# Leaky-ReLU taken twice from the PSUM accumulator by ScalarE, and GpSimd's elementwise work given to VectorE, in a dynamic convolution followed by two MLPs

## The chip, the cores and the metric

One NeuronCore of a Trainium2 chip runs the whole program in one launch. The metric is the device time of that launch in microseconds; the program before was run three times.

## The reference

```python
# local sum: softmax over 7 taps per token and head, then a causal weighted sum
w = exp(weight_gen - max(weight_gen, -1)); w = w / (sum(w, -1) + 1e-9)
x_pad = concatenate([zeros(B, 6, D), x], axis=1)
out = einsum('bshk,bskhg->bshg', w, x_unf)       # B=2, S=4096, D=192, 8 heads, 7 taps
x = out.reshape(8192, 192)
# first MLP: leaky ReLU with slope 0.01
h = x @ moe_w_in;  g = maximum(0.01 * h, h);  x = g @ moe_w_out       # 192 -> 2048 -> 192
# second MLP: squared ReLU
h = x @ moe2_w_in; r = maximum(h, 0); g = r * r; out = g @ moe2_w_out # 192 -> 2048 -> 192
```

The weights arrive as float64 words, and are turned into float32 on the core.

## The kernel before, in words

**Tiles.** The 8192 tokens are worked in 16 blocks of 512 (`NTB`), the 2048 hidden features in 16 slices of 128 (`NFC`). A *step* is one block and one slice of one layer: 512 steps in all. A *phase* is the 16 steps of one block in one layer. The phases run in the order layer 1 block 0 (steps 0 to 15), layer 1 block 1 (16 to 31), layer 2 block 0 (32 to 47), layer 1 block 2 (48 to 63), layer 2 block 1, and so on alternately. In the code layer 1 is `l == 0`.

**Exact halves.** Each float32 operand v of a product is split into two float32r halves: h is v rounded, and lo is v minus h. Products are summed as h*h + h*lo + lo*h.

**One step.** `mm1` (L376) makes the hidden slice in a PSUM tile `ph` (two buffers) by five matmuls. `act_a` applies the activation: in layer 1 ScalarE copies `ph` to `g` (L383) and VectorE replaces `g` by max(0.01 g, g) (L384); in layer 2 ScalarE does Relu from `ph` and Square in place (L386, L387). One step later `act_b` makes the two halves: `gh`, a rounding copy of `g`, on ScalarE (L395) or VectorE (L397), swapped for the steps listed in `GH_SWAP`; and `gl = g - gh` (L398) on VectorE, or on GpSimd for the 35 steps in `GL_POOL`, all below step 44. Three steps after the activation (`LAG`) `mm2` (L411 to L415 for layer 1, L425 and L428 for layer 2) multiplies `gh` and `gl` by the output weights. `g` has three buffers, `gh` and `gl` four.

**The weights.** 28 pieces of weights (14 a layer; kinds a, b of the input matrix and o of the output matrix) are prepared among steps 0 to 45, at the steps in `DUE`. A piece is loaded by DMA; ScalarE scales its high words (`scale`, L138); VectorE joins them by four instructions (`join`: L151, L154, L155, L147) and an add (L148) that is VectorE's or GpSimd's by the table `ENGINES`; then `split` makes the halves: h by ScalarE or VectorE (L163), lo = v minus h by VectorE or GpSimd (L164). The three numbers of a piece in `ENGINES` are for the add, lo and h; 0 is GpSimd for the first two and ScalarE for the third, 1 is VectorE.

**The local sum.** Of each of the first three blocks (`POOL_TAPS`) taps 0 to 3 are multiplied and added by VectorE (L269, L295) and taps 4 to 6 by GpSimd (`pool_mul`, `pool_add`: L269, L280); the last addition (L295) joins them. Later blocks have all taps on VectorE.

**Order.** Nothing reorders instructions: the main loop of the kernel writes out, step by step, which instruction each engine gets next, and every engine takes its own in that order, each waiting for what it reads and for the buffer it writes. In a step the order is: first part of the next piece's join, `act_b` of the step before, second part, `mm1`, `mm2` of three steps before, `act_a`, `split` of the piece that is due, `scale` of the piece two further on, then parts of the local sum and the rest of the join.

Of the kernel before, what the change touches and what calls it, by code (L numbers as in the profile page):

```python
# [9 lines left out]
F32R = mybir.dt.float32r  # L10
# [5 lines left out]
ALU = mybir.AluOpType  # L16
AX = mybir.AxisListType

# The places of the weights' and the first local sums' parts among the steps.
ORDER = [['b0', 'a0', 'o0', 'a1', 'o3', 'o1', 'o2', 'b1', 'a2', 'a3', 'o4', 'o5', 'o6', 'o7'], ['a0', 'o1', 'b0', 'o0', 'b1', 'a2', 'a1', 'o3', 'o2', 'a3', 'o4', 'o5', 'o7', 'o6']]  # L20
DUE = [[-2, -1, 1, 2, 3, 4, 5, 6, 7, 8, 9, 11, 12, 13], [18, 20, 22, 24, 28, 29, 30, 33, 36, 38, 39, 40, 44, 45]]
ENGINES = [[1, 0, 0], [1, 1, 1], [0, 0, 0], [1, 0, 0], [0, 0, 0], [0, 0, 0], [1, 0, 0], [0, 0, 0], [1, 0, 0], [0, 1, 0], [0, 1, 0], [0, 0, 0], [0, 0, 1], [1, 0, 1], [0, 0, 1], [1, 1, 0], [0, 0, 0], [0, 0, 0], [1, 0, 1], [0, 0, 1], [1, 0, 1], [1, 0, 1], [0, 0, 1], [0, 0, 0], [1, 0, 0], [1, 1, 1], [1, 0, 1], [1, 1, 0]]
POOL_TAPS = [3, 3, 3]
CONV_AT = [[0, 1, 4, 5, 6, 6, 7, 7, 8, 8, 10, 11, 12, 14, 14], [0, 0, 1, 4, 8, 8, 10, 13, 17, 18, 25, 26, 26, 28, 30]]
SIDE_AT = [[0, 1, 3, 4, 5, 6, 7, 8, 9, 10, 12, 14], [0, 1, 3, 4, 10, 11, 15, 17, 19, 20, 21, 22]]
GL_POOL = [0, 1, 2, 3, 4, 5, 7, 8, 10, 11, 12, 13, 14, 15, 17, 18, 19, 20, 21, 22, 23, 25, 26, 27, 28, 29, 30, 32, 33, 35, 37, 38, 39, 40, 43]
GH_SWAP = [0, 12, 14, 16, 17, 18, 22, 26, 31, 32, 33, 34, 35, 39, 40, 41, 44, 45, 47]


# [1 line left out]
def kernel(  # L31
# [7 lines left out]
    w_out2: bass.AP,  # L39
    out: bass.AP,  # L40
):
    # Every float32 operand of a product is split exactly into two float32r
    # halves of 12 significant bits, v = h + l, and each product is summed from
    # single-pass float32r products h*h + h*l + l*h (+ l*l where it comes free).
    # Token n sits on partition n // 64; block t of 128 tokens is {64 p + t}.
    nc = tc.nc
    w_in1, w_out1, w_in2, w_out2 = (
        w.bitcast(I32).rearrange("r (c w) -> r c w", w=2) for w in (w_in1, w_out1, w_in2, w_out2)
# [37 lines left out]

    ident = const.tile([P, P], F32, name="ident")

    # ---------------------------------------------------------------- weights
    wi = []  # L90
    for l in range(2):
        wi.append(
# [10 lines left out]
    }  # L103
    wo2 = const.tile([P, NFC, 2 * D], F32R, name="wo2")

    # float64 words -> the nearest float32. u, the high word read as a float32
    # times 2**-112, has in its 11 upper bits under the sign the float64's
    # exponent less 8 * 112 (what lies below 2**-119 runs out towards zero), so
    # moved left by 3 it is the float32 of the upper 20 fraction bits; the low
    # word times 2**-52 and the power of two of the value is the rest.  # L110
    # A piece goes through four stages.
    class Piece:
        def __init__(self, kind, l, c):
            self.kind, self.l, self.c = kind, l, c
# [68 lines left out]
                else:  # L183
                    halves(wo2[:, fs, 0:D], wo2[:, fs, D : 2 * D], r)

    # The step before whose products a piece is done, in the order of need.
    pieces = [
        (d, Piece(k[0], l, int(k[1:]))) for l in range(2) for d, k in zip(DUE[l], ORDER[l])
    ]
# [1 line left out]
        p.feng, p.leng, p.heng = ENGINES[q]  # L191
    due = dict(pieces)

    # -------------------------------------------------- softmax and local sum
    x_flat = x.rearrange("b (p t) d -> (b p) t d", t=TPP)
    wg_flat = weight_gen.rearrange("b (p t) h k -> (b p) t h k", t=TPP)
    out_flat = out.rearrange("(p t) d -> p t d", t=TPP)
# [62 lines left out]
    def conv_steps(tb):  # L260
        c, o = divmod(tb * TB, CH)
        steps = list(softmax_steps(c)) if o == 0 else []
        att = cv.tile([P, TB, 2 * P], F32, name="att", tag="att", bufs=1)
        acc = att[:, :, 0:D].rearrange("p t (h g) -> p t h g", g=G)

        def prod(k, dst, eng=nc.vector):
            xk = xc_t[c][:, o + k : o + k + TB, :].rearrange("p t (h g) -> p t h g", g=G)
            wk = wn_t[c][:, o : o + TB, :, k : k + 1]
            eng.tensor_tensor(dst, xk, wk.to_broadcast([P, TB, H, G]), op=ALU.mult)  # L269

        tmps = {}
        kv = K - PTAPS.get(tb, 0)
        side = []

        def pool_mul(k):
            tmps[k] = xt.tile([P, TB, H, G], F32, name="tmp", tag="ot" if k == kv else "o2", bufs=1)
            prod(k, tmps[k], nc.gpsimd)

        def pool_add(k):
            nc.gpsimd.tensor_tensor(tmps[kv], tmps[kv], tmps.pop(k), op=ALU.add)  # L280

        for k in range(kv, K):
            side.append(lambda k=k: pool_mul(k))
            if k > kv:
                side.append(lambda k=k: pool_add(k))
        side_t[tb] = side

        def mul(k):
            tmps[k] = cv.tile([P, TB, H, G], F32, name="tmp", tag="tmp")
            prod(k, tmps[k])  # L290

        def add(k, last):
            while last and side:
                side.pop(0)()
            nc.vector.tensor_tensor(acc, acc, tmps.pop(k), op=ALU.add)  # L295
            if last and tb < 3:
                nc.scalar.copy(att[:, :, D : 2 * P], att[:, :, DA:D])

        steps.append(lambda: prod(0, acc))
        for k in range(1, kv):  # L300
            steps.append(lambda k=k: mul(k))
            steps.append(lambda k=k: add(k, k == K - 1))
        if kv < K:
            steps.append(lambda: add(kv, True))

        xs = x1_t[tb] = {}

        def tr(half):
            if tb != 1 and not (tb == 2 and PH3):
                pt = ps_ab.tile([P, N], F32, name="pt", tag=("pa", "pb")[half])  # L310
            else:
                pt = ps_o.tile([P, N], F32, name="pt", tag=f"po{half}")
            for t in range(TB):
                nc.tensor.transpose(pt[:, t * P : (t + 1) * P], att[:, t, half * P : (half + 1) * P], ident)
            h, l = (("ah", "al"), ("bh", "bl"))[half]
            for k in (h, l):
                xs[k] = half_tile(X1SET(tb), k)
            nc.scalar.copy(xs[h], pt)
            nc.vector.tensor_tensor(xs[l], pt, xs[h].bitcast(F32), op=ALU.subtract)  # L319

        def blocks():
            J = D // 32
            xb = st.tile([P, J, TB, 32], F32, name="xb", tag="raw", bufs=3)
            nc.vector.transpose(
                xb.rearrange("p j t a -> p t j a"), att[:, :, 0:D].rearrange("p t (j b) -> p t j b", b=32)
            )
            sc = dram.tile([P, J * N // 4], F32, name="sc", tag="sc")
            nc.sync.dma_start(out=sc, in_=xb.rearrange("p j t a -> p (j t a)"))
            xa = st.tile([P, N], F32, name="xa", tag="wu", bufs=3)
            xbb = st.tile([P, N], F32, name="xbb", tag="wa", bufs=3)  # L330
            for j in range(J + 2):
                dst, k = (xa, j) if j < 4 else (xbb, j - 4)
                q = j if j < J else j - 2
                nc.sync.dma_start(
                    out=dst[32 * k : 32 * k + 32].rearrange("b (i m) -> b i m", i=4),
                    in_=sc.rearrange("(i b) (j m) -> j b i m", b=32, j=J)[q],
                )
            tmps["x"] = xa, xbb

        def fr(half):  # L340
            v = tmps["x"][half]
            h, l = (("ah", "al"), ("bh", "bl"))[half]
            for k in (h, l):
                xs[k] = half_tile(X1SET(tb), k)
            nc.scalar.copy(xs[h], v)
            nc.vector.tensor_tensor(xs[l], v, xs[h].bitcast(F32), op=ALU.subtract)

        def shift():
            if c + 2 < NCH:
                load_chunk(c + 2)  # L350

        if o == CH - TB:
            steps.append(shift)
        if tb < 3:
            steps.append(lambda: tr(0))
            steps.append(lambda: tr(1))
        else:
            steps.append(blocks)
            steps.append(lambda: fr(0))
            steps.append(lambda: fr(1))  # L360
        return steps

    # ------------------------------------------------------------------- MLPs
    x2_t = {}
    g_t = {}
    h_t = {}
# [12 lines left out]
    def act_a(l, tb, fc):  # L379
        ph = h_t.pop((l, tb, fc))  # L380
        g = gp.tile([P, N], F32, name="g", tag="g", bufs=3)
        if l == 0:
            nc.scalar.copy(g, ph)  # L383
            nc.vector.scalar_tensor_tensor(g, g, 0.01, g, op0=ALU.mult, op1=ALU.max)  # L384
        else:
            nc.scalar.activation(g, ph, AF.Relu)  # L386
            nc.scalar.activation(g, g, AF.Square)  # L387
        h_t[l, tb, fc] = g

    def act_b(l, tb, fc, eng, gh_dve):  # L390
        g = h_t.pop((l, tb, fc))
        gh = gp.tile([P, N], F32R, name="gh", tag="gh")
        gl = gp.tile([P, N], F32R, name="gl", tag="gl")
        if (l == 0) != gh_dve:
            nc.scalar.copy(gh, g)  # L395
        else:
            nc.vector.tensor_copy(gh, g)  # L397
        eng.tensor_tensor(gl, g, gh.bitcast(F32), op=ALU.subtract)  # L398
        g_t[l, tb, fc] = gh, gl

# [72 lines left out]
            phases += [(0, tb), (1, tb - 1)]  # L473
        phases.append((1, NTB - 1))

    # Slots of the steps at which the parts of a local sum come: 0.. in the L1
    # phase before, NFC.. in the L2 phase that follows it.
    def plan(fs, tb):
        if tb < 2 + PH3:
            at = CONV_AT[tb]  # L480
# [119 lines left out]
```

## Time and profile before

| what | value |
|---|---|
| three runs | 1317.88, 1316.14, 1316.87 us; median 1316.87 us |
| profiled execution: span | 1317.7 us; no other time of that execution is given, the median of the runs is 0.8 us under its span |
| busy in that span | PE 1222.1 us (93%), VectorE (DVE) 1020.9 (77%), ScalarE (ACT) 692.1 (53%), GpSimd (POOL) 137.8 (10%, 100 instructions) |
| chain of work that ended last | PE 83%, DVE 13%, issue 3%, DMA 1% |

Busy time is the time in which an engine had an instruction under way. Shares over the whole span hide that the program has two stages: one in which the weights are prepared and GpSimd works, and the rest. The same views are therefore read stage by stage.

### The profile page before, as it was taken

How to read it: one execution, taken by the hardware profiler on the slowest of the kernel's cores; microseconds unless marked ns; L12 is line 12 of the kernel's file. 1: busy time of each engine (PE TensorE's matmuls, PEld its weight loads, DVE VectorE, ACT ScalarE, POOL GpSimd, SP SyncE). 2: the span in 40 equal slices, each digit the busy share in tenths (PEclk: the TensorE clock that was granted, in tenths of full speed). 3: DMA queues.
4: the chain of work that ended last, by engine and by line, in shares of the span. 5: the costliest groups of instructions: out<-in, count | busy, mean ns of one | idle time of the engine just before them, and what ended most of it. 6: DMA issues, size and time to landing. Idle time of an engine off the chain costs nothing.

```text
span 1317.7 us, 16605 instructions
## 1 busy us (share of the span) xinstructions
PE 1222.1 (93%) x5912; PEld 1026.1 (78%) x5912; DVE 1020.9 (77%) x1599; ACT 692.1 (53%) x1224; POOL 137.8 (10%) x100
## 2 busy tenths in 40 slices
PE   0648678999999999999999999999999999999997
PEld 0436456888888988888888988888888988888897
DVE  7999999787867777787867777787867777786553
ACT  1423345555555555555555555555555555555554
POOL 4666764000000000000000000000000000000000
PEclk9869989999999999999999999999999999999999
DMA  5332222020110102020110102020110101010000
GB/s 146 113 98 64 64 76 70 12 68 15 41 41 9 62 13 70 13 70 13 40 43 8 62 13 70 13 68 15 34 48 9 62 13 37 13 32 17 9 12 13
DMA packets 41123, 55.72 MB, mean 42 GB/s; under 512 B 4178, under 2 KB 30290, under 8 KB 41040
## 3 DMA queue, kind: packets, MB, share of 16 engines
q1 hardware_dynamic: 41040, 54.66, 13.8%
q8 instruction: 46, 0.75, 0.2%
q14 instruction: 37, 0.30, 0.1%
HBM read 28.11 MB, written 11.40 MB: 30 GB/s over the span
## 4 chain that ended last, share of the span: by engine, by line
PE 83%; DVE 13%; issue 3%; DMA 1%; POOL 0%; ACT 0%; SPq 0%; DVEq 0%
PE ph L376 42%; PE po L425 14%; PE po L428 7%; PE pb L413 4%; PE pa L415 4%; PE pa L412 4%; PE pa L411 4%; PE pb L414 4%; DVE wa L154 2%; DVE wu L147 1%; DVE g L384 1%; DVE wa L151 1%; DVE wu L155 1%; DVE tmp L269 1%; DVE att L295 1%
## 5 line engine op out<-in xcount | busy, mean ns | idle before, releaser
L398 DVE TENSOR_TENSOR gl<-g,gh 128x512 fp32r<-128x512 f32 x478 | 333.8, 698 | 112.8 <-ACT gh L395 87.2
L425 PE MATMUL po<-wo,gh 128*128 128x384 f32 x1024 | 307.6, 355 | 0.5 <-DVE gh L397 0.3
L395 ACT CAST gh<-g 128x512 fp32r<-128x512 f32 x256 | 158.6, 620 | 222.7 <-DVE g L384 222.6
L428 PE MATMUL po<-wo,gl 128*128 128x192 f32 x1024 | 257.5, 251 | 5.3 <-POOL gl L398 3.6
L386 ACT ACTIVATE g<-ph 128x512 f32<-128x512 f32 x256 | 153.2, 598 | 193.0 <-PE ph L376 185.6
L384 DVE SCALAR_TENSOR_TENSOR g<-g 128x512 f32<-128x512 f32 x256 | 198.4, 775 | 32.7 <-ACT g L383 30.9
L428 PEld LDWEIGHTS po<-wo,gl 128*128 128x128 f32 x1024 | 195.5, 191 | 18.1 <-POOL gl L398 5.0
L425 PEld LDWEIGHTS po<-wo,gh 128*128 128x128 f32 x1024 | 192.9, 188 | 13.4 <-DVE gh L397 0.9
L383 ACT COPY g<-ph 128x512 f32<-128x512 f32 x256 | 149.4, 585 | 59.9 <-PE ph L376 58.7
L387 ACT ACTIVATE g<-g 128x512 f32<-128x512 f32 x256 | 162.0, 633 | 8.2
L397 DVE CAST gh<-g 128x512 fp32r<-128x512 f32 x256 | 111.6, 436 | 66.9 <-ACT g L387 66.7
L376 PE MATMUL ph<-xah,wi0ah 128*128 128x512 f32 x256 | 105.1, 411 | 22.5 <-ACT wi0ah L163 11.9
L414 PE MATMUL pb<-gl,wo1b 128*128 128x512 f32 x256 | 103.8, 405 | 8.9 <-POOL gl L398 8.1
L411 PE MATMUL pa<-gh,wo1ah 128*128 128x512 f32 x256 | 103.7, 405 | 6.5 <-ACT wo1ah L163 5.0
L412 PE MATMUL pa<-gh,wo1al 128*128 128x512 f32 x256 | 103.2, 403 | 6.7 <-DVE wo1al L164 3.5
L376 PE MATMUL ph<-xah,wi1ah 128*128 128x512 f32 x256 | 104.8, 409 | 3.4 <-ACT g L386 2.4
L376 PE MATMUL ph<-xbl,wi0b 128*128 128x512 f32 x256 | 103.4, 404 | 2.1 <-DVE xbl L319 2.1
L376 PE MATMUL ph<-xah,wi0al 128*128 128x512 f32 x256 | 103.6, 404 | 1.6 <-POOL wi0al L164 1.6
L413 PE MATMUL pb<-gh,wo1b 128*128 128x512 f32 x256 | 103.8, 405 | 0.6 <-DVE wo1b L164 0.5
L415 PE MATMUL pa<-gl,wo1ah 128*128 128x512 f32 x256 | 103.2, 403 | 0.0
L376 PE MATMUL ph<-xal,wi0ah 128*128 128x512 f32 x256 | 102.4, 400 | 0.0
L376 PE MATMUL ph<-xbh,wi0b 128*128 128x512 f32 x256 | 102.3, 400 | 0.0
(92 smaller groups left out, 1817.6 us busy)
## 6 DMA issues: line engine op xcount, KB each, us to landing
xc<-xc SPq DMA_DIRECT2D x15, 576.0 KB
xc<-in_x_dram SPq DMA_DIRECT2D x16, 384.0 KB
raw<-in_moe_w_out_dram SPq DMA_DIRECT2D x16, 384.0 KB
sc<-xb SPq DMA_DIRECT2D x13, 384.0 KB
out_dram<-ot SPq DMA_DIRECT2D x52, 96.0 KB
raw<-in_moe_w_in_dram SPq DMA_DIRECT2D x8, 512.0 KB
bw<-bs SPq DMA_DIRECT2D x32, 128.0 KB
xa<-sc SPq DMA_DIRECT2D x52, 64.0 KB
```

What stands on the lines that cost most here:

```text
L376: nc.tensor.matmul(ph, lhsT=w[a][:, fs], rhs=xs[b], start=(i == 0), stop=(i == len(terms) - 1))
L384: nc.vector.scalar_tensor_tensor(g, g, 0.01, g, op0=ALU.mult, op1=ALU.max)
L387: nc.scalar.activation(g, g, AF.Square)
L395: nc.scalar.copy(gh, g)
L398: eng.tensor_tensor(gl, g, gh.bitcast(F32), op=ALU.subtract)
L411: nc.tensor.matmul(pa, lhsT=wo1["ah"][:, fc, :], rhs=gh, start=first, stop=False)
L412: nc.tensor.matmul(pa, lhsT=wo1["al"][:, fc, :], rhs=gh, start=False, stop=False)
L413: nc.tensor.matmul(pb, lhsT=wo1["b"][:, fc, :], rhs=gh, start=first, stop=False)
L414: nc.tensor.matmul(pb, lhsT=wo1["b"][:, fc, :], rhs=gl, start=False, stop=last)
L415: nc.tensor.matmul(pa, lhsT=wo1["ah"][:, fc, :], rhs=gl, start=False, stop=last)
L425: nc.tensor.matmul(po, lhsT=gh[:, ts], rhs=wo2[:, fc, :], start=first, stop=False, skip_group_check=True)
L428: nc.tensor.matmul(po[:, 0:D], lhsT=gl[:, ts], rhs=wo2[:, fc, 0:D], start=False, stop=last, skip_group_check=True)
```

## The change

Four edits, none of which moves an instruction to another step:

1. In layer 1 `act_a` issues two ScalarE activations from `ph`, both Prelu with slope 0.01: one writes `g` in float32, one writes `gh` rounded to float32r. VectorE's leaky ReLU (L384) and the rounding copies of layer 1 (L395, L397) are gone, and `gh` of layer 1 is allocated one step earlier, in `act_a`.
2. `GL_POOL` is empty: `gl` of every step is VectorE's.
3. `ENGINES` is [1, 1, 0] for all 28 pieces: the add and lo are VectorE's, h is ScalarE's.
4. `pool_mul` and `pool_add` are issued on VectorE, at the same places.

```diff
-ENGINES = [[1, 0, 0], [1, 1, 1], [0, 0, 0], [1, 0, 0], [0, 0, 0], ...
+ENGINES = [[1, 1, 0]] * 28
-GL_POOL = [0, 1, 2, 3, 4, 5, 7, 8, 10, 11, 12, 13, 14, 15, 17, ...
+GL_POOL = []
...
         def pool_mul(k):
             tmps[k] = xt.tile([P, TB, H, G], F32, name="tmp", tag="ot" if k == kv else "o2", bufs=1)
-            prod(k, tmps[k], nc.gpsimd)
+            prod(k, tmps[k])
 
         def pool_add(k):
-            nc.gpsimd.tensor_tensor(tmps[kv], tmps[kv], tmps.pop(k), op=ALU.add)
+            nc.vector.tensor_tensor(tmps[kv], tmps[kv], tmps.pop(k), op=ALU.add)
...
         if l == 0:
-            nc.scalar.copy(g, ph)
-            nc.vector.scalar_tensor_tensor(g, g, 0.01, g, op0=ALU.mult, op1=ALU.max)
+            gh = gp.tile([P, N], F32R, name="gh", tag="gh")
+            nc.scalar.activation(g, ph, AF.Prelu, alpha=0.01)
+            nc.scalar.activation(gh, ph, AF.Prelu, alpha=0.01)
+            h_t[l, tb, fc] = g, gh
+            return
...
     def act_b(l, tb, fc, eng, gh_dve):
-        g = h_t.pop((l, tb, fc))
-        gh = gp.tile([P, N], F32R, name="gh", tag="gh")
+        if l == 0:
+            g, gh = h_t.pop((l, tb, fc))
+        else:
+            g = h_t.pop((l, tb, fc))
+            gh = gp.tile([P, N], F32R, name="gh", tag="gh")
+            if gh_dve:
+                nc.scalar.copy(gh, g)
+            else:
+                nc.vector.tensor_copy(gh, g)
         gl = gp.tile([P, N], F32R, name="gl", tag="gl")
-        if (l == 0) != gh_dve:
-            nc.scalar.copy(gh, g)
-        else:
-            nc.vector.tensor_copy(gh, g)
         eng.tensor_tensor(gl, g, gh.bitcast(F32), op=ALU.subtract)
```

In the changed program the Prelus are L384 and L385, the rounding copies of layer 2 L400 and L402, and `gl` is L404.

VectorE's queue around step 1, before (`wa`, `wu` belong to a piece of weights, `wg` to the softmax, `g`, `gh`, `gl` to the hidden slice):

```order
L151 TENSOR_SCALAR wa<-wu 128x512
L154 SCALAR_TENSOR_TENSOR wa<-wu,wa 128x512
L384 SCALAR_TENSOR_TENSOR g<-g 128x512
L155 TENSOR_SCALAR wu<-wa 128x512
L234 TENSOR_TENSOR wg<-wg,mx 128x224
L147 SCALAR_TENSOR_TENSOR wu<-raw,wu 128x512
L148 TENSOR_TENSOR wa<-wa,wu 128x512
L151 TENSOR_SCALAR wa<-wu 128x384
```

and the same place of the changed program:

```order
L151 TENSOR_SCALAR wa<-wu 128x512
L404 TENSOR_TENSOR gl<-g,gh 128x512
L154 SCALAR_TENSOR_TENSOR wa<-wu,wa 128x512
L164 TENSOR_TENSOR wo1al<-wa,wo1ah 128x256
L164 TENSOR_TENSOR wo1b<-wa,wo1b 128x2x64
L155 TENSOR_SCALAR wu<-wa 128x512
L234 TENSOR_TENSOR wg<-wg,mx 128x224
L147 SCALAR_TENSOR_TENSOR wu<-raw,wu 128x512
L148 TENSOR_TENSOR wa<-wa,wu 128x512
L151 TENSOR_SCALAR wa<-wu 128x384
```

The leaky ReLU has left the queue; the lo parts of the piece that is due and `gl` of the step before have come in from GpSimd.

ScalarE's queue in steps 2 and 3, before:

```order
L395 CAST gh<-g 128x512
L383 COPY g<-ph 128x512
L163 CAST wi0ah<-wa 128x512
L138 ACTIVATE wu<-raw 128x384
L395 CAST gh<-g 128x512
L383 COPY g<-ph 128x512
L163 CAST wo1ah<-wa 128x256
L163 CAST wo1b<-wa 128x2x64
L138 ACTIVATE wu<-raw 128x384
```

and now:

```order
L384 ACTIVATE g<-ph 128x512
L385 ACTIVATE gh<-ph 128x512
L163 CAST wi0ah<-wa 128x512
L138 ACTIVATE wu<-raw 128x384
L384 ACTIVATE g<-ph 128x512
L385 ACTIVATE gh<-ph 128x512
L163 CAST wo1ah<-wa 128x256
L163 CAST wo1b<-wa 128x2x64
L138 ACTIVATE wu<-raw 128x384
```

A step still gives ScalarE two passes over the hidden slice, now side by side and both from `ph`; the rounding copy no longer reads what VectorE made. GpSimd's queue, which before held rows like these at the same steps,

```order
L148 TENSOR_TENSOR wa<-wa,wu 128x384
L398 TENSOR_TENSOR gl<-g,gh 128x512
L164 TENSOR_TENSOR wo1al<-wa,wo1ah 128x256
L164 TENSOR_TENSOR wo1b<-wa,wo1b 128x2x64
L398 TENSOR_TENSOR gl<-g,gh 128x512
L164 TENSOR_TENSOR wi0al<-wa,wi0ah 128x512
```

keeps only its memsets and the identity matrix at the start.

## Rows read from the trace of the kernel before

**Rows 1.** The page's 40 slices of the span: busy tenths, granted clock.

```profile
DVE  7999999787867777787867777787867777786553
POOL 4666764000000000000000000000000000000000
PEclk9869989999999999999999999999999999999999
```

**Rows 2.** Two stretches: length, busy us (instructions) of PE, PEld, DVE, ACT, POOL; clock, DMA.

```profile
11.09:232.83 221.74, 144.77 (x542) 105.04 (x543) 217.41 (x259) 85.33 (x163) 134.76 (x92) 0.88 0.28 85
232.83:1317.70 1084.87, 1077.33 (x5371) 921.09 (x5369) 801.32 (x1335) 604.89 (x1058) 0.00 (x0) 1.00 0.11 32
```

**Rows 3.** Timeline of PE, first matmul of two successive layer 1 steps.

```profile
608.41 0.41 PE L376 MATMUL ph<-xah,wi0ah 128*128 128x512 f32 x1
...
610.76 0.39 PE L376 MATMUL ph<-xah,wi0ah 128*128 128x512 f32 x1
```

**Rows 4.** DVE's groups from 11.09 to 232.83 us: busy us, mean ns, idle before.

```profile
L384 DVE SCALAR_TENSOR_TENSOR g<-g 128x512 f32<-128x512 f32 x33 | 44.6, 1353 | 1.1 <-ACT g L383 1.1
L154 DVE SCALAR_TENSOR_TENSOR wa<-wu,wa 128x512 int32<-128x512 int32 x12 | 14.7, 1229 | 0.2
...
L398 DVE TENSOR_TENSOR gl<-g,gh 128x512 fp32r<-128x512 f32 x14 | 13.8, 988 | 0.4
...
L319 DVE TENSOR_TENSOR xal<-pt,xah 128x512 fp32r<-128x512 f32 x3 | 2.0, 683 | 0.0
...
L231 DVE TENSOR_REDUCE mx<-wg 128x32 f32<-128x224 f32 x2 | 0.8, 380 | 0.0
```

**Rows 5.** DVE's groups from 500 to 1300 us.

```profile
L398 DVE TENSOR_TENSOR gl<-g,gh 128x512 fp32r<-128x512 f32 x346 | 238.7, 690 | 83.3 <-ACT gh L395 63.8 <-DVE gh L397 0.5
L384 DVE SCALAR_TENSOR_TENSOR g<-g 128x512 f32<-128x512 f32 x160 | 110.3, 690 | 23.3 <-ACT g L383 22.0
L397 DVE CAST gh<-g 128x512 fp32r<-128x512 f32 x186 | 78.4, 422 | 52.4 <-ACT g L387 52.4
L269 DVE TENSOR_TENSOR tmp<-xc,wg 128x768 f32<-128x768 f32 x56 | 53.3, 952 | 0.0
```

**Rows 6.** Timeline of DVE: start, us; first and last row bound the stage.

```profile
11.09 0.96 DVE L269 TENSOR_TENSOR att<-xc,wg 128x768 f32<-128x768 f32 x1 [5.62 <-DMA xc<-in_x_dram]
...
46.93 0.68 DVE L384 SCALAR_TENSOR_TENSOR g<-g 128x512 f32<-128x512 f32 x1
...
49.94 1.77 DVE L384 SCALAR_TENSOR_TENSOR g<-g 128x512 f32<-128x512 f32 x1
...
232.83 0.69 DVE L384 SCALAR_TENSOR_TENSOR g<-g 128x512 f32<-128x512 f32 x1
```

**Rows 7.** Timeline of POOL in the same microseconds.

```profile
45.21 1.38 POOL L164 TENSOR_TENSOR wi0al<-wa,wi0ah 128x512 fp32r<-128x512 f32 x1
48.55 1.05 POOL L148 TENSOR_TENSOR wa<-wa,wu 128x384 f32<-128x384 f32 x1 [1.96 <-DVE wu L147]
49.57 1.60 POOL L398 TENSOR_TENSOR gl<-g,gh 128x512 fp32r<-128x512 f32 x1
```

**Rows 8.** POOL's two costliest groups from 11 to 232.83 us.

```profile
L398 POOL TENSOR_TENSOR gl<-g,gh 128x512 fp32r<-128x512 f32 x34 | 53.4, 1573 | 17.1 <-DVE gh L397 7.0 <-PE ph L376 6.2 <-ACT gh L395 3.8
L269 POOL TENSOR_TENSOR tmp<-xc,wg 128x768 f32<-128x768 f32 x9 | 18.6, 2066 | 9.4 <-DMA xc<-in_x_dram 7.4 <-DVE wg L243 1.9
```

**Rows 9.** The page's costliest groups: three of ScalarE's passes over the hidden slice.

```profile
L395 ACT CAST gh<-g 128x512 fp32r<-128x512 f32 x256 | 158.6, 620 | 222.7 <-DVE g L384 222.6
L386 ACT ACTIVATE g<-ph 128x512 f32<-128x512 f32 x256 | 153.2, 598 | 193.0 <-PE ph L376 185.6
L383 ACT COPY g<-ph 128x512 f32<-128x512 f32 x256 | 149.4, 585 | 59.9 <-PE ph L376 58.7
```

**Rows 10.** Timeline of ACT where a layer 1 phase has just begun.

```profile
607.75 1.18 ACT L453 COPY ot<-po 128x192 f32<-128x192 f32 x4 [0.61 <-PE po L428]
608.82 0.59 ACT L383 COPY g<-ph 128x512 f32<-128x512 f32 x1
```

More of the change, by code (lines that the diff above doesn't have):

```diff
@@ L21 @@
 DUE = [[-2, -1, 1, 2, 3, 4, 5, 6, 7, 8, 9, 11, 12, 13], [18, 20, 22, 24, 28, 29, 30, 33, 36, 38, 39, 40, 44, 45]]
-ENGINES = [[1, 0, 0], [1, 1, 1], [0, 0, 0], [1, 0, 0], [0, 0, 0], [0, 0, 0], [1, 0, 0], [0, 0, 0], [1, 0, 0], [0, 1, 0], [0, 1, 0], [0, 0, 0], [0, 0, 1], [1, 0, 1], [0, 0, 1], [1, 1, 0], [0, 0, 0], [0, 0, 0], [1, 0, 1], [0, 0, 1], [1, 0, 1], [1, 0, 1], [0, 0, 1], [0, 0, 0], [1, 0, 0], [1, 1, 1], [1, 0, 1], [1, 1, 0]]
+ENGINES = [[1, 1, 0]] * 28
 POOL_TAPS = [3, 3, 3]
@@ L25 @@
 SIDE_AT = [[0, 1, 3, 4, 5, 6, 7, 8, 9, 10, 12, 14], [0, 1, 3, 4, 10, 11, 15, 17, 19, 20, 21, 22]]
-GL_POOL = [0, 1, 2, 3, 4, 5, 7, 8, 10, 11, 12, 13, 14, 15, 17, 18, 19, 20, 21, 22, 23, 25, 26, 27, 28, 29, 30, 32, 33, 35, 37, 38, 39, 40, 43]
+GL_POOL = []
 GH_SWAP = [0, 12, 14, 16, 17, 18, 22, 26, 31, 32, 33, 34, 35, 39, 40, 41, 44, 45, 47]
```

## Prediction

> **What bounds the kernel now.** Over the whole span PE is the busy engine, but the slices say that there are two stages [rows 1]: seven slices in which GpSimd works and VectorE is nearly full, and thirty-three without GpSimd. I take as their border the start of VectorE's activation of step 48, at 232.83 us; the last weights are ready by then, and VectorE's work on blocks begins at 11.09 us [rows 6]. Cut there, PE is busy 144.8 of 221.7 us in the first stage and VectorE 217.4; in the rest PE is busy 1077.3 of 1084.9 [rows 2], at full clock, and two successive layer 1 steps start 2.35 us apart [rows 3], which is ten matmuls with nothing between them. So the rest is bound by PE, and nothing that ScalarE or VectorE save there shows; I leave its 1084.9 us as they are. **The first stage is bound by VectorE**, idle for only 4.3 us of it, and the whole change has to be priced there, on VectorE's queue.
>
> Next I ask why VectorE is so slow there. The same instruction on 512 elements takes 1353 ns (L384) and 988 ns (L398) in the first stage [rows 4], 690 ns later [rows 5]. The timeline shows the cause: the L384 that starts at 46.93, when GpSimd's instruction has just ended at 46.59, takes 0.68 us; the one at 49.94, which starts 0.37 us into a GpSimd instruction of 1.60 us, takes 1.77 [rows 6, 7]. VectorE stands until GpSimd's instruction is over, then does its own. Not every kind is caught: the subtraction that has one operand in PSUM (L319) stays at 683 ns and the reduction (L231) at 380 in the midst of it [rows 4]; had DMA or something general been the cause, they would be longer too.
>
> **Clean prices.** For two-operand work on 768 and 512 elements 0.952 and 0.690 us [rows 5]; the straight line through them gives 0.559, 0.428 and 0.297 for 384, 256 and 128. A rounding copy of 512 takes 0.422 [rows 5]; for the one-operand instructions of the join (L151, L155) I take the same, and 0.356 for 384.
>
> **The stage as it is, at clean prices.** The 259 instructions that VectorE has there [rows 2] are, by the order: 24 of 768 elements (22.8 us), 91 of 512 with two operands (62.8), 43 of 384 (24.0), 47 one-operand of 512 (19.8), 36 of 384 (12.8), and 18 small ones of the softmax and the split (6.1): 148.3 us. All groups of the view of rows 4 add up to 232.1 us, while the engine is busy 217.4 [rows 2]: neighbours overlap, by 0.057 us each. So waiting for GpSimd lengthens the instructions by 232.1 - 148.3 = **83.8 us**. Check: 148.3 - 14.7 overlap + 83.8 + 4.3 idle = 221.7.
>
> **What the change does to that queue.** Everything GpSimd does after its set-up, 92 instructions and 134.8 us [rows 2], comes over: 34 `gl` and 16 other instructions of 512 elements (34.5 us at clean price, where GpSimd needs 1.57 us for one [rows 8]), 15 products and sums of 768 (14.3; GpSimd 2.07 each [rows 8]), 13 of 384 (7.3), 7 of 256 and 7 of 128 (5.1): +61.2. Away go 33 activations (22.8), 9 rounding copies of layer 1 (3.8) and 13 of weights (4.5): -31.1. That leaves 296 instructions, 148.3 + 61.2 - 31.1 = 178.4 us, less 296 overlaps of 0.057 (16.9): **161.5 us of work**, with no GpSimd to wait for. The moved work costs 61; it removes 84 of waiting.
>
> **Idle time that comes in.** (a) Start: lo of the piece a0 now stands right behind its add, so VectorE waits for ScalarE's rounding (0.62 [rows 9]), then for that of the first block's transposed input: 2 us. (b) In the light steps PE becomes the bound. Priced as above, VectorE's steps 12 to 15 hold 6.8 us and steps 40 to 47 15.6, PE's 9.3 and 18.7 at 2.33 us a step: 5.6 us more. (c) 4.5 us for lo parts that wait for a rounding copy; mostly L151, `gl` and L154, 1.8 us together, stand between add and lo and hide it. Together 12. The stage then takes 173.5 us, ends at 184.6, and the span is 184.6 + 1084.9 = 1269.5; less the 0.8 us by which the median of the runs lies under the span, **1269 us**, 48 us or 3.6% faster. PE does not stand in the way of that: 48 steps of 2.33 us from 32 us on would be done by 145.
>
> **ScalarE.** Prelu does not occur in the trace. Nearest below is the copy from `ph` (585 ns), above two passes (1.2 us); I take Relu from `ph`, 598 [rows 9], since it is the same kind of instruction. A layer 1 step then has 1.20 us of activation where it had 585 + 620, so ScalarE's sum does not change, and its second pass no longer waits for L384, on which it now waits 222.6 us in all [rows 9]. The 13 roundings that it takes over are 6 us in a stage in which it is busy 85 of 222 [rows 2]: hidden by its idle time. The accumulator is held for two passes instead of one. The tables are loaded once in the changed order too, so Prelu adds no load. DMA: no transfer is added or moved; the shift of the b pieces waits for lo, which comes sooner.
>
> **A rule against it.** The activation leaves VectorE, 0.690 us at clean price, for ScalarE, which needs 1.20 for it and the rounding [rows 5, 9]. The Trainium skill, ScalarE: Activation LUTs, Rules for kernel authors, says the opposite: relu, max and multiplication belong on VectorE, not on ScalarE. By that rule the 33 activations would stay in the full queue, the stage would be 22.8 us longer and the gain 25 us instead of 48. The rows decide for the change, because ScalarE is idle for more than half of this stage and VectorE is not.
>
> **The rivals.**
> 1. *VectorE waits for ScalarE at every lo.* GpSimd was late without holding anybody's queue; now each of the 28 pieces can stop VectorE for a rounding and its signal, 0.7 us, and each light step runs at PE's pace with no borrowing between neighbours (13 us in place of 5.6): idle 35 in place of 12, so 1292 us. Against it: the three instructions in between.
> 2. *The accumulator becomes the bound.* Two buffers of `ph`: at 2.33 us a step a matmul group starts one and a half steps, 3.5 us, after the end of the one whose buffer it takes, and two passes fill 1.2 of that. Where ScalarE first empties the output, the activation starts 1.1 us late [rows 10] and nothing is left over: up to 1 us in each of 15 phases, 1284 us. The Trainium skill, VectorE: DVE Perf Modes, Rules for kernel authors, would have a matmul result copied to SBUF first if much is done on it; the kernel before does that. Against it: PE has 1077 of 1085 us filled, and ScalarE is the one that waits, for PE, before L386 and L383 [rows 9].
> 3. *Prelu is slow* (the slower side). If it takes p, a layer 1 step needs 2p + 0.18 us of ScalarE with its share of the other copies; at p over 1.08 that exceeds PE's 2.33. At 1.2, as with a second pass for the negative side, each of the 224 layer 1 steps after the first stage costs 0.25 us: +56 us, 1325. Against it: three different passes over 512 elements take 585, 598 and 620 ns [rows 9].
> 4. *The long instructions are not GpSimd's doing* (also slower). Then they stay long and 61 us at the long prices come in: the 296 at the first stage's means are 260 us, the stage 247, and the time 1342. It turns slower from 48 us of waiting that remain. Rows 4, 6 and 7 speak against it.
>
> **How the numbers follow.** Within the forecast (70%) the idle time lies between the present 4 and some 24 us: 1261 to 1281. Rival 1 (and slow stretches of PE's clock, which stands at 0.6 to 0.9 in the first seven slices [rows 1], of the same size) 17%, rival 2 6%, rival 3 3%, rival 4 2%, other 2%. The range 1258 to 1295 holds the forecast and rivals 1 and 2. Anything under 0.2% (2.6 us) a measurement of this kernel would not tell from no change. Faster 0.94, same 0.01, slower 0.05.
>
> **What would show it.** In the changed profile: no GpSimd after 4 us; L404 and L154 on 512 elements at 0.69 us from the start; the `gl` of step 47 done at about 185 us, where before the next activation starts at 232.8 [rows 6]; the rest 1085 us; Prelu at 0.60. Wrong would be: VectorE idle for over 25 us before that point, waiting for L163 (rival 1); PE waiting for L385 after it (rival 2); Prelu over 1 us (rival 3); a VectorE instruction of 512 elements over 1 us (rival 4).

## The result, and the profile after

The changed kernel takes 1263.02 us (median of 4 runs, 1262.33 to 1264.31); the kernel before 1317.38 (median of 4, three of them the runs given above). The ratio of the two is 0.9584, with a 95% interval of 0.9571 to 0.9598: 54.4 us faster, where 48 were forecast. The time lies in the forecast's range.

The 40 slices of the changed kernel's page, which answer to [rows 1]:

```profile
span 1260.8 us, 16315 instructions
...
DVE  7999975757566575756657575665757556573453
...
POOL 0000000000000000000000000000000000000000
PEclk9899999999999999999999999999999999999999
```

GpSimd is gone, and VectorE's full stretch has shrunk from seven slices to five. The two stages, cut as in [rows 2]: from VectorE's first product to the end of `gl` of step 47, and the rest (length; busy us of PE, PEld, DVE, ACT, POOL; clock, DMA share, GB/s):

```profile
8.07:175.54 167.47, 129.79 (x539) 101.55 (x540) 160.41 (x297) 93.19 (x186) 0.00 (x0) 0.94 0.39 115
175.54:1260.80 1085.26, 1077.92 (x5375) 922.31 (x5374) 660.15 (x1110) 582.91 (x1059) 0.00 (x0) 1.00 0.11 32
```

**The whole gain lies in the first stage**: 221.7 us before, 167.5 now. The rest took 1084.9 and takes 1085.3, although VectorE does 141 us less in it (801.3 to 660.2): PE bounds it, as before. In the first stage VectorE is busy 160.4 us; it was priced at 161.5. Its groups there (11 to 185 us), against [rows 4]:

```profile
L404 DVE TENSOR_TENSOR gl<-g,gh 128x512 fp32r<-128x512 f32 x52 | 35.5, 685 | 2.9 <-ACT gh L385 2.2 <-ACT gh L400 0.2
L269 DVE TENSOR_TENSOR tmp<-xc,wg 128x768 f32<-128x768 f32 x16 | 15.1, 952 | 0.1
...
L148 DVE TENSOR_TENSOR wa<-wa,wu 128x384 f32<-128x384 f32 x16 | 8.9, 558 | 0.6
...
L154 DVE SCALAR_TENSOR_TENSOR wa<-wu,wa 128x512 int32<-128x512 int32 x12 | 8.2, 684 | 0.0
...
L164 DVE TENSOR_TENSOR wi0al<-wa,wi0ah 128x512 fp32r<-128x512 f32 x4 | 2.7, 686 | 0.7 <-ACT wi0ah L163 0.7
...
L319 DVE TENSOR_TENSOR xal<-pt,xah 128x512 fp32r<-128x512 f32 x3 | 2.1, 689 | 0.6 <-ACT xah L318 0.6
```

Every two-operand instruction of 512 elements shown here is at 0.69 us (L154 was at 1229 ns, `gl` at 988), and those of 768 and 384 at the 0.952 and 0.56 that the prediction used. L319, which had never been long, is where it was. ScalarE's passes on the page, against [rows 9]:

```profile
L384 ACT ACTIVATE g<-ph 128x512 f32<-128x512 f32 x256 | 153.5, 600 | 248.0 <-PE ph L376 246.8
...
L385 ACT ACTIVATE gh<-ph 128x512 fp32r<-128x512 f32 x256 | 152.3, 595 | 0.0
```

Prelu costs 600 and 595 ns, and the second pass waits for nothing: the 222.6 us for which the rounding copy stood waiting for VectorE are gone. What ScalarE waits for before L384 is PE (246.8 of 248.0 us).

### The profile page after: what moved, and what is told of

It reads as the page before. It is cut to its first block, busy times and chain, and to the rows that moved or that the text cites. A ratio compares the mean times of both kernels' runs of the same rounds, so it can differ in the third digit from the quotient of the medians.

```text
span 1260.8 us, 16315 instructions
## 1 busy us (share of the span) xinstructions
PE 1207.7 (96%) x5912; PEld 1023.9 (81%) x5912; DVE 822.7 (65%) x1413; ACT 678.0 (54%) x1246; POOL 2.8 (0%) x8
## 4 chain that ended last, share of the span: by engine, by line
PE 89%; DVE 8%; issue 1%; ACT 1%; DMA 0%; SPq 0%; DVEq 0%
PE ph L376 45%; PE po L431 15%; PE po L434 7%; PE pa L417 4%; PE pb L419 4%; PE pa L421 4%; PE pb L420 4%; PE pa L418 4%; DVE tmp L269 1%; DVE gl L404 1%; DVE wu L147 1%; DVE wa L154 1%; DVE wa L148 1%; DVE att L295 1%; DVE wu L155 1%
## 5 line engine op out<-in xcount | busy, mean ns | idle before, releaser
L404 DVE TENSOR_TENSOR gl<-g,gh 128x512 fp32r<-128x512 f32 x512 | 353.5, 691 | 260.9 <-ACT gh L385 232.9
L384 ACT ACTIVATE g<-ph 128x512 f32<-128x512 f32 x256 | 153.5, 600 | 248.0 <-PE ph L376 246.8
L389 ACT ACTIVATE g<-ph 128x512 f32<-128x512 f32 x256 | 153.1, 598 | 198.7 <-PE ph L376 198.7
L402 DVE CAST gh<-g 128x512 fp32r<-128x512 f32 x247 | 104.1, 422 | 79.2 <-ACT g L390 79.2
L385 ACT ACTIVATE gh<-ph 128x512 fp32r<-128x512 f32 x256 | 152.3, 595 | 0.0
L376 PE MATMUL ph<-xbl,wi1b 128*128 128x512 f32 x256 | 102.1, 399 | 0.0
```

What stands on the lines that cost most here:

```text
L376: nc.tensor.matmul(ph, lhsT=w[a][:, fs], rhs=xs[b], start=(i == 0), stop=(i == len(terms) - 1))
L384: nc.scalar.activation(g, ph, AF.Prelu, alpha=0.01)
```

## Experiments

Times are medians; a ratio is that median over the one of the kernel before in the same group of runs, with its 95% interval in brackets. The kernel before took 1317.7 us beside the first three experiments and the one on the accumulator, 1318.4 beside the copies, the point between and the run with less for VectorE, and 1317.8 beside the last two. Since the input lands between 8 and 11 us from one profile to the next, the profiles are compared by the time from VectorE's first product to PE's first matmul of step 48: 219.2 us before (11.09 to 230.28), 165.5 in the changed kernel (8.07 to 173.60).

**One part alone: the activation.** The three edits on GpSimd's work are undone.

```diff
-ENGINES = [[1, 1, 0]] * 28
+ENGINES = [[1, 0, 0], [1, 1, 1], [0, 0, 0], ...
-GL_POOL = []
+GL_POOL = [0, 1, 2, 3, 4, 5, 7, 8, ...
-            prod(k, tmps[k])
+            prod(k, tmps[k], nc.gpsimd)
-            nc.vector.tensor_tensor(tmps[kv], tmps[kv], tmps.pop(k), op=ALU.add)
+            nc.gpsimd.tensor_tensor(tmps[kv], tmps[kv], tmps.pop(k), op=ALU.add)
```

> Only the activation changes: Prelu twice on ScalarE, GpSimd keeps all its work. Theory (VectorE's queue bounds the first stage, and its instructions wait for GpSimd's): 33 activations and 9 rounding copies leave the queue, 26.6 us at clean prices less 42 overlaps of 0.057, while GpSimd still works 135 us and still stops VectorE; 24 us faster than before if the 84 us of waiting stay, up to 38 if they shrink with the number of instructions: 1279 to 1293 us. Rival (the gain of the change came from the shorter chain through ScalarE, whose second pass no longer waits for VectorE): nearly the whole gain is here, about 1265 us, and the run with only GpSimd's work moved shows little.

Measured: 1295.64 us, ratio 0.983 (0.9814 to 0.9846): 22 us faster, a little less than the range said. VectorE's groups before (11.09 to 232.83 us) and in this run (8 to 210 us) show where the rest of the expected gain went:

```profile
L154 DVE SCALAR_TENSOR_TENSOR wa<-wu,wa 128x384 int32<-128x384 int32 x16 | 14.4, 898 | 0.4
...
L155 DVE TENSOR_SCALAR wu<-wa 128x384 int32<-128x384 int32 x16 | 10.8, 676 | 0.2
```

```profile
L154 DVE SCALAR_TENSOR_TENSOR wa<-wu,wa 128x384 int32<-128x384 int32 x16 | 16.4, 1023 | 0.4
...
L155 DVE TENSOR_SCALAR wu<-wa 128x384 int32<-128x384 int32 x16 | 14.1, 884 | 0.4
```

They went from 898 to 1023 ns and from 676 to 884. The 33 activations had borne 22 us of the waiting (1353 ns each where the clean price is 690); without them other instructions bear it. Taken over all groups, at the clean prices of the prediction, which the changed kernel confirmed, waiting is 80.7 us here and 84.3 before: it did not shrink with the number of instructions. The rival, by which nearly the whole gain would have come from the shorter chain through ScalarE, is out.

**The other part alone: GpSimd's work.** The kernel before, with `GL_POOL` empty, `ENGINES` all [1, 1, 0] and the taps on VectorE.

```diff
-ENGINES = [[1, 0, 0], [1, 1, 1], [0, 0, 0], ...
+ENGINES = [[1, 1, 0]] * 28
-GL_POOL = [0, 1, 2, 3, 4, 5, 7, 8, ...
+GL_POOL = []
-            prod(k, tmps[k], nc.gpsimd)
+            prod(k, tmps[k])
-            nc.gpsimd.tensor_tensor(tmps[kv], tmps[kv], tmps.pop(k), op=ALU.add)
+            nc.vector.tensor_tensor(tmps[kv], tmps[kv], tmps.pop(k), op=ALU.add)
```

> Only GpSimd's work moves to VectorE (with the weights' roundings on ScalarE, as in the change); copy, leaky ReLU and rounding copy stay as before. Theory: 148.3 + 61.2 - 4.5 = 205 us of clean work, less 338 overlaps of 0.057 is 186, with 6 to 12 us idle a stage of 192 to 198 in place of 221.7: 24 to 30 us faster than before, 1287 to 1293 us, and no VectorE instruction of 512 elements over 1 us. Rival (long instructions are not GpSimd's doing): slower than before, 1340 us or so. Rival (chain through ScalarE): within 10 us of before.

Measured: 1283.86 us, ratio 0.9744 (0.973 to 0.9759): 34 us faster, 4 more than the range. Up to step 48 it needs 185.5 us, 33.7 less than before. Its stage, and two of VectorE's groups in it (8 to 200 us):

```profile
8.48:196.00 187.52, 133.41 (x540) 100.45 (x541) 181.49 (x337) 91.20 (x176) 0.00 (x0) 0.93 0.35 103
```

```profile
L398 DVE TENSOR_TENSOR gl<-g,gh 128x512 fp32r<-128x512 f32 x50 | 34.3, 686 | 2.5 <-ACT gh L395 1.1
L384 DVE SCALAR_TENSOR_TENSOR g<-g 128x512 f32<-128x512 f32 x34 | 23.2, 683 | 1.1 <-ACT g L383 1.1
```

VectorE has more instructions than ever, 337, no long one among them, and is 6.0 us idle: giving it GpSimd's 92 instructions, and taking only 13 roundings of weights off it, made the kernel faster. The two parts give 21.3 and 33.7 us up to step 48; together they gave 53.7, nearly their sum. This run is also the version in which the activation stays on VectorE: 21 us slower than the change.

**GpSimd works, and nobody needs it.** The changed kernel; at the old steps GpSimd computes `gl` once more, into a spare tile that nobody reads. The 35 entries of the old `GL_POOL` stand for 34 instructions, here as before: at entry 0 no slice has been made yet.

```diff
         eng.tensor_tensor(gl, g, gh.bitcast(F32), op=ALU.subtract)
+        if ghost:
+            spare = xt.tile([P, N], F32, name="spare", tag="spare", bufs=1)
+            nc.gpsimd.tensor_tensor(spare, g, gh.bitcast(F32), op=ALU.subtract)
```

> The changed kernel, and beside it GpSimd computes the 35 old gl once more into a tile that nobody reads, at the old steps; no result waits for it. Theory: GpSimd has 53 us of such work, 40% of what it had, so VectorE waits for some 0.4 x 84 = 33 us again: the first stage is 25 to 40 us longer than in the changed kernel, 1288 to 1303 us, and VectorE instructions of 512 elements over 1 us come back. Rival (what cost time was the results coming late from GpSimd, not its running): the time of the changed kernel within 3 us, 1263 us.

Measured: 1295.07 us, ratio 0.9826 (0.9812 to 0.9841), 32 us over the changed kernel. Lateness of results cannot be the reason, since nobody reads them; and the buffers that the useless instruction keeps occupied made another engine wait only once (ScalarE, 1.9 us). GpSimd's group, and two of VectorE's (8 to 210 us; line numbers are one higher in this file and the next, so L155 is L154 of the changed kernel, L320 its L319):

```profile
L408 POOL TENSOR_TENSOR spare<-g,gh 128x512 f32<-128x512 f32 x34 | 52.8, 1552 | 141.5 <-ACT gh L386 112.7 <-ACT gh L401 12.7 <-DVE gh L403 12.6
```

```profile
L155 DVE SCALAR_TENSOR_TENSOR wa<-wu,wa 128x384 int32<-128x384 int32 x16 | 13.1, 821 | 0.0
...
L320 DVE TENSOR_TENSOR xal<-pt,xah 128x512 fp32r<-128x512 f32 x3 | 2.1, 688 | 0.6 <-ACT xah L319 0.6
```

L155 of 384 elements goes from 0.552 to 0.821 us, L320 stays. Summed as above, VectorE waits 32.0 us for GpSimd's 52.8.

**The same with a copy.** GpSimd's useless instruction reads one tile instead of two.

```diff
-            nc.gpsimd.tensor_tensor(spare, g, gh.bitcast(F32), op=ALU.subtract)
+            nc.gpsimd.tensor_copy(spare, g)
```

> As the run with the ghost gl, but GpSimd's useless instruction is a copy with one input. Theory A (what stops VectorE is GpSimd's use of SBUF, whatever it computes): VectorE waits for 0.6 of the copies' busy time, so 34 copies of 0.6 to 1.2 us make the time 12 to 25 us longer than the changed kernel, 1275 to 1288 us. Theory B (only two-input instructions of GpSimd stop VectorE): the changed kernel's time within 3 us, 1263 us, with no long VectorE instruction.

Measured: 1275.91 us, ratio 0.9682 (0.9668 to 0.9696): 13 us over the changed kernel. One-input instructions stop VectorE too, but less in proportion:

```profile
L408 POOL COPY spare<-g 128x512 f32<-128x512 f32 x34 | 30.8, 906 | 140.7 <-ACT g L385 113.9 <-ACT g L391 26.6
```

VectorE waits 11.1 us for these 30.8: 0.33 us for each of the 34 copies, where each subtraction cost 0.94 (32.0 / 34). The timelines show why. The same three instructions with the subtraction (first) and with the copy (second), rows of VectorE and GpSimd:

```profile
174.21 0.69 DVE L405 TENSOR_TENSOR gl<-g,gh 128x512 fp32r<-128x512 f32 x1
174.27 1.78 POOL L408 TENSOR_TENSOR spare<-g,gh 128x512 f32<-128x512 f32 x1 [5.32 <-DVE gh L403]
174.82 1.78 DVE L155 SCALAR_TENSOR_TENSOR wa<-wu,wa 128x512 int32<-128x512 int32 x1
```

```profile
157.62 0.69 DVE L405 TENSOR_TENSOR gl<-g,gh 128x512 fp32r<-128x512 f32 x1
157.65 1.14 POOL L408 COPY spare<-g 128x512 f32<-128x512 f32 x1 [2.82 <-ACT g L391]
158.23 1.10 DVE L155 SCALAR_TENSOR_TENSOR wa<-wu,wa 128x512 int32<-128x512 int32 x1
```

In both, L155 ends 0.54 to 0.55 us after GpSimd's instruction, at a clean price of 0.684: what differs is how long it stood before that. And GpSimd waits as well: its subtraction ends 1.15 us after the `gl` that was under way when it started, its copy 0.48 us after. It is so at every such place of the two runs: 1.12 to 1.16 us (21 subtractions), 0.47 to 0.48 (23 copies). So a subtraction can stop VectorE for about 1.0 us and a copy for about 0.33 (0.14 less than those times), and the rest of GpSimd's recorded time is its own waiting, or costs VectorE nothing: its subtractions took 1.27 to 2.67 us, its copies 0.61 to 2.13.

**A point between.** The changed kernel with the weights' work and the three taps back on GpSimd, `gl` on VectorE.

```diff
-ENGINES = [[1, 1, 0]] * 28
+ENGINES = [[1, 0, 0], [1, 1, 1], [0, 0, 0], ...
-            prod(k, tmps[k])
+            prod(k, tmps[k], nc.gpsimd)
-            nc.vector.tensor_tensor(tmps[kv], tmps[kv], tmps.pop(k), op=ALU.add)
+            nc.gpsimd.tensor_tensor(tmps[kv], tmps[kv], tmps.pop(k), op=ALU.add)
```

> The changed kernel with only gl on VectorE: the weights' work and the three taps stay on GpSimd, 58 instructions and 81 us. If waiting is 0.62 us for each us that GpSimd works (83.8 of 134.8 before, 32 of 53 with the ghosts): clean work 178.4 - 37.7 + 4.5 = 145.2, waiting 50, overlaps 14.3, 6 idle: a stage of 187 us, 20 us more than the changed kernel's 167.5, so 1283 us. Rival (waiting goes with the number of VectorE's instructions, so the first 53 us of GpSimd were the bad ones): under 1275 us.

Measured: 1282.23 us, ratio 0.9729 (0.9713 to 0.9745), where 1283 was expected. Its stage (GpSimd's 80.62 us stand last of the busy times):

```profile
9.57:197.00 187.43, 133.94 (x542) 102.82 (x543) 178.66 (x252) 89.23 (x173) 80.62 (x58) 0.92 0.35 102
```

The runs in a line; waiting is the sum of VectorE's durations in the stage less the same instructions at clean prices, the ratio is waiting over GpSimd's busy time:

| kernel | GpSimd busy in the stage, us | VectorE's waiting, us | ratio |
|---|---|---|---|
| before | 134.8 | 84.3 | 0.63 |
| activation alone | 131.6 | 80.7 | 0.61 |
| `gl` on VectorE | 80.6 | 47.2 | 0.59 |
| useless `gl` | 52.8 | 32.0 | 0.61 |
| useless copies | 30.8 | 11.1 | 0.36 |
| the change | 0 | under 1 | |

The ratio is no constant of GpSimd's work. Busy time less waiting, divided by the number of GpSimd's instructions (92, 92, 58, 34, 34), is 0.55 to 0.61 us in all five rows: a short instruction costs VectorE a smaller share of its time.

**The accumulator, read once.** The changed kernel, with the rounding from SBUF.

```diff
-            nc.scalar.activation(gh, ph, AF.Prelu, alpha=0.01)
+            nc.scalar.copy(gh, g)
```

> The changed kernel with the second Prelu replaced by a rounding copy of g from SBUF, so that the accumulator is free after one pass. Theory: the accumulator's second pass is hidden everywhere, so the time of the changed kernel within 2 us (a copy takes 0.62 us, a Prelu from the accumulator 0.595). Rival (the accumulator held for two passes stops PE): 3 to 10 us faster than the changed kernel, with PE's waits for L385 gone.

Measured: 1265.15 us (1262.8 to 1266.68), ratio 0.9598 (0.9584 to 0.9613), against the changed kernel's 0.9584 (0.9571 to 0.9598): the intervals overlap, and its median is the higher one. Up to step 48 it needs 165.7 us to the change's 165.5. Holding the accumulator for two passes costs nothing that can be seen; in either kernel the view of the waits has none of PE's after 176 us.

**Less for VectorE in steps 32 to 47.** ScalarE makes `gh` of all layer 2 steps there.

```diff
-    GH = set(GH_SWAP)
+    GH = set(GH_SWAP) | set(range(32, 49))
```

> The changed kernel with gh of all layer 2 steps 32 to 47 made by ScalarE (seven more than now). Theory: VectorE still bounds the first stage (busy 160.4 of 167.5 us), so 7 x 0.42 less 7 x 0.057 = 2.5 us come off it, and ScalarE (busy 93 of 167) hides 7 x 0.62: 1260 to 1261.5 us against 1263.0, the best of all. Rival (PE or the chain through ScalarE bounds steps 32 to 47 by now): the time of the changed kernel within 1 us, or up to 3 us slower where gl waits for ScalarE.

Measured: 1264.89 us, ratio 0.96 (0.9586 to 0.9614): no gain, a miss. Up to step 48 it is 166.3 us against 165.5. But the steps that the edit touches did become shorter. The first matmul of step 32 and that of step 48, in this run and in the changed kernel:

```profile
130.87 0.50 PE L376 MATMUL ph<-xah,wi1ah 128*128 128x512 f32 x1
...
175.37 0.41 PE L376 MATMUL ph<-xah,wi0ah 128*128 128x512 f32 x1
```

```profile
127.26 0.50 PE L376 MATMUL ph<-xah,wi1ah 128*128 128x512 f32 x1
...
173.60 0.41 PE L376 MATMUL ph<-xah,wi0ah 128*128 128x512 f32 x1
```

That is 44.5 us where the changed kernel takes 46.3 (46.0 in its second profile): 1.5 to 1.8 us less, of the 2.5 expected. The loss stands before them, where the two programs are the same: at step 32 this run is 2.6 us behind. In step 14 PE's granted clock was at half (1.2 GHz) here and at full (2.4 GHz) there; the same 6.8 us of the two runs, 1 us apart as their input landed 1 us apart:

```profile
80.80:87.60 6.80, 5.93 (x18) 4.86 (x19) 5.46 (x13) 4.29 (x11) 0.00 (x0) 0.50 0.21 58
```

```profile
79.80:86.60 6.80, 5.93 (x30) 4.93 (x31) 6.34 (x15) 5.27 (x14) 0.00 (x0) 1.00 0.20 58
```

PE was busy equally long and did 18 matmuls in place of 30. Before that PE had stood for the same three waits in both (0.48, 0.73 or 0.74, and 1.56 us). So this run does not show that relieving VectorE in these steps is useless; whether the clock also fell in its other three executions, whose times lie within 0.5 us of each other, no profile shows, and why there was no gain stays open to that extent.

**Another order, to gain more.** In the changed kernel the local sum of the second block comes two to three steps later, behind the weights of steps 5 to 9.

```diff
-CONV_AT = [[0, 1, 4, 5, 6, 6, 7, 7, 8, 8, 10, 11, 12, 14, 14], ...
+CONV_AT = [[0, 1, 4, 5, 8, 9, 9, 10, 11, 11, 12, 13, 13, 14, 14], ...
-SIDE_AT = [[0, 1, 3, 4, 5, 6, 7, 8, 9, 10, 12, 14], ...
+SIDE_AT = [[8, 9, 10, 11, 12], ...
```

> The changed kernel with the local sum of the second block two to three steps later (its products from step 8 instead of 6, the former GpSimd taps in steps 8 to 12), so that the weights of steps 5 to 9 come first. Theory: VectorE bounds steps 0 to 12 and PE the steps after; VectorE's steps 5 to 8 then hold 4.2 to 4.9 us instead of 4.9 to 6.7, PE gets its weights sooner and lies less behind at step 13: 1 to 4 us faster than the changed kernel run beside it. Rival (VectorE's sum up to step 16 is all that counts, it is unchanged): within 1 us.

Measured: 1267.35 us, ratio 0.9621 (0.9608 to 0.9635), 5 us slower than the changed kernel beside it. On PE's timeline the transposes of the second block now stand waiting (the second fence is the changed kernel beside it):

```profile
86.34 1.97 PE L314 MATMUL pt<-ident,att 128*128 128x128 f32 x8 [5.35 <-DVE att L295]
87.96 0.78 PE L376 MATMUL ph<-xah,wi0ah 128*128 128x512 f32 x1
```

```profile
84.06 1.03 PE L314 MATMUL pt<-ident,att 128*128 128x128 f32 x8
84.85 0.48 PE L376 MATMUL ph<-xah,wi0ah 128*128 128x512 f32 x1
```

PE takes its instructions in order, and the transposes stand in step 14. Up to there the earlier weights had gained more than was expected: counted from the first product, step 14 begins 5.1 us sooner than in the changed kernel. That was lost by standing 5.35 us for the sum. Some 3 us more (an estimate from the same matmuls at either clock) went because PE's granted clock was at half from 76.5 to 79.9 us, after a wait of 1.60 us, and fell to half again during the wait for the sum:

```profile
83.30:90.10 6.80, 3.76 (x13) 3.38 (x14) 5.41 (x10) 3.06 (x7) 0.00 (x0) 0.50 0.48 181
```

In the same microseconds of the changed kernel it is 1.00, with 34 matmuls. Step 48 begins 4.1 us later (169.3 against 165.2). Both theories are wrong about the whole: neither a gain nor no difference.

**The change once more**, beside the run just told.

> The changed kernel itself on the chip of the run with the taps later, to have both side by side: 1263 us, within 2 us of its earlier median, and 8 to 10 us for the first product of the local sum, which starts when the input has landed (8.07 us in its first profile, 11.09 before the change).

Measured: 1262.36 us (1260.99 to 1264.96), ratio 0.9582 (0.9569 to 0.9595). The first product starts at 9.07 us, and step 48 begins 165.2 us later. No version tried beats the change.

## Why the prediction was right, point by point

**What bounds what.** Right. The rest after step 48 is PE's, 1085.3 us against 1084.9, and the useless `gl` and the moved `gl` show that time put on VectorE in the first stage is time of the kernel.

**84 us of waiting.** Right in cause and size, and in mechanism: a VectorE instruction of 512 elements and two operands that is caught ends some 0.55 us after GpSimd's, 0.14 less than it takes by itself. It is the running of GpSimd that costs VectorE time, not the lateness of its results: 52.8 us of results that nobody reads cost 32. The kinds that are caught fit a page of the Trainium skill, GPSIMD Engine Reference, Specifications: GpSimd shares its SBUF interfaces with VectorE, and they contend with VectorE instructions that read two SBUF operands or run in a two-port mode. The traces agree: L154, with two SBUF operands, was at 1229 ns; L319, with one of its two in PSUM, was at 683 and the reduction at 380 in the same stage [rows 4]. Of the instructions with one SBUF operand some are caught too: L155 of 384 elements was at 676 ns and is at 356 in the changed kernel; in which mode it runs, no trace shows.

**61 us of moved work, 31 us taken off.** Right: 161.5 us of work forecast, 160.4 busy measured. The same prices also gave the run with only `gl` moved to within 1 us.

**Idle time, 12 us.** This is the term that was mis-sized: 167.47 - 160.41 = 7.1 us, which with the 1.1 us of work makes the stage 167.5 where 173.5 was forecast, and the gain 54 where 48 was. The start, (a), was 2 us and shows as 1.6 on VectorE's timeline (0.69 and 0.23 us for the first lo and xal, 0.40 and 0.23 for the next scale and lo). The lo parts, (c), were put at 4.5 us, and hardly wait: L151, `gl` and L154 cover them, and beside the two at the start one wait of 0.8 us for a rounding is left. Light steps, (b), put at 5.6 us, are where the forecast was wrong in kind. The changed kernel's steps 12 to 15 and 40 to 47:

```profile
72.54:86.32 13.78, 11.01 (x49) 8.23 (x48) 13.22 (x29) 6.63 (x17) 0.00 (x0) 1.00 0.40 133
149.76:173.60 23.84, 21.35 (x115) 18.76 (x113) 23.17 (x47) 17.81 (x34) 0.00 (x0) 0.93 0.24 80
```

VectorE is busy 13.2 of 13.8 and 23.2 of 23.8 us there, where its own work in these steps was priced at 6.8 and 15.6: it is still working off what had piled up, so PE does not bound these steps, and 1.2 us are idle. Of the 7.1 us, 3 stand in gaps of under 0.12 us all over the stage, which no term of the sum had. The rival built on (c) is out.

**The span.** 1260.8 us against 1269.5: 6.0 from the stage, and 3.0 because the input landed at 8.07 us in this profile and at 11.09 before. The step from span to time had the wrong sign. Where both are known of one execution, the time is 1.7 to 2.1 us above the span (1262.62 for 1260.8), not 0.8 below it; the median of the runs before and that span came from different executions. So the forecast by its own terms was some 1271 us, and the runs, not the spans, give the gain: 54.4 us, of which 53.7 are seen between the first product and step 48.

**ScalarE and the rule.** Prelu was put at 598 ns and costs 600 and 595, so the slow Prelu is out, and nothing is seen of a cost of the accumulator. (The rival on it counted wrongly: of 3.5 us, two passes of 1.2 and a start 1.1 late leave 1.2 over, not nothing.) The rule of the Trainium skill, ScalarE: Activation LUTs, Rules for kernel authors, puts relu and max on VectorE. With the activation kept there the gain was priced at 25 us: the run that keeps it gains 34, and is 21 slower than the change. The rule did not hold here, where VectorE bounds the stage and ScalarE has idle time. The 4 us by which that run beat its range are less work, 181.5 us busy where 186 was put (overlaps of 0.063 us instead of 0.057 are 2 of them), with idle time, 6.0 us, at the low end of the 6 to 12 expected.

## What to carry to other kernels

Before giving elementwise work to GpSimd, price what VectorE loses by it: here each GpSimd subtraction of 512 elements stopped a busy VectorE for 0.94 us, more than the 0.69 of doing it itself, and each copy for 0.33. Look for it by comparing one instruction's mean duration between stages with and without GpSimd; a busy VectorE may be a waiting one. Take work off the engine that bounds the stage, to an idle one, even if each instruction costs more there. And before calling a change useless, compare the two profiles stretch by stretch, the granted clock beside them: a loss can stand where the programs are the same.

## What the runs showed that was not expected

Waiting does not shrink with the number of VectorE's instructions: with 41 fewer it fell only from 84.3 to 80.7 us, and the remaining ones became longer. It follows GpSimd's instructions, all but some 0.6 us of each. The two engines stop each other: whichever of two such instructions starts first, the other one ends a fixed time after it. Steps that were light on paper were not light when VectorE came to them. Why the input lands between 8 and 11 us was left open.
